# A cached-attention decode kernel: values three groups behind the keys in the load order, and the whole output projection after the last attention group

## The chip, the cores and the metric

The kernel runs on one core of one Trainium2 chip. The metric is the device time of one execution in microseconds. A run counts as slow when it is over 1.5% above the fastest of its kernel. The a runs, the b runs and the c and d runs were made on three different chips; the kernel before was timed beside them each time, at 195.54, 195.39, 195.54 and 195.57 us.

Ratios are means of the fast runs of one kernel over means of the other's in the same call. They are not quite the ratios of the medians that are quoted beside them.

## The reference, cut to what matters

```python
# attention for one new token: B=8, Hq=16, Hkv=8, Dh=256; only the last W=1024 keys count
q = (x @ wq) ...                                    # x [8,448], wq [448,4096]
scores = einsum("bhqd,bhkd->bhqk", q, k) * Dh**-0.5
p = softmax(scores); o = einsum("bhqk,bhkd->bhqd", p, v)
a = o.reshape(B, 1, 4096) @ wo                      # wo [4096,448]
# an MLP on the same x (w1 [448,1792], w2 [1792,448]), and a gate from x and gate_w
out = g * a + (1 - g) * b
```

Keys and values are 8 x 8 x 1024 x 256 bf16 each, 33.5 MB and 33.5 MB. With the weights, 77.68 MB have to be read once, and nothing is used twice. There is little arithmetic per byte.

## The kernel before

The 64 pairs of batch and kv head are cut into 16 groups of four. A group's keys are one slot of 2 MB, its values another. A ring of nine slots is filled by one queue, strictly in the order of `plan`; a slot's next load is issued when the slot has been read.

```python
    RING = 9
    ...
    def pump():
        while len(slots) < min(len(plan), consumed[0] + RING):
            t = ring.tile([P, SLOT], BF16, tag="slot", name="slot")
            plan[len(slots)](t)            # nc.sync.dma_start(...)
            slots.append(t)
    ...
    add_kv("k", A_k_cache, 0, parts=2)     # then w1, wq (two slots), w2
    ...
    for u in range(1, NQ - 1):             # NQ = 16 groups
        add_kv("k", A_k_cache, u)
        if u < NQ - 2:
            add_kv("v", A_v_cache, u - 1)
    add_kv("k", A_k_cache, NQ - 1)
    for u in range(NQ - 3, NQ):
        add_kv("v", A_v_cache, u)
    # then wo: quarters 0 and 1 in one slot, quarters 2 and 3 in the next;
    # quarter 3 is loaded in three pieces, so that the last one is small (224 KB)
```

So the stream ends: key 14, key 15, values 13, 14, 15, output weights. The work on a group is: `transpose_keys` (64 TensorE transposes, copied out by ScalarE and VectorE, with the softmax of the group before woven in), `scores` (16 matmuls), `top` (the maximum), and for an older group `values` (32 matmuls) and `finish` (a fold into `oT`, four matmuls in the trace). `expo`, `turn` and `bring` are the three steps of a group's softmax: exponentials on ScalarE, a transpose on VectorE, and matmuls that put the result in order for `values`.

```python
    for u in range(1, NQ - 1):
        transpose_keys(u, steps(u - 1))
        if u < NQ - 2:
            values(u - 1)
        scores(u)
        top(u)
        if u < NQ - 2:
            finish(u - 1)
    u = NQ - 1
    transpose_keys(u, steps(u - 1))
    scores(u)
    top(u)
    values(u - 2)
    finish(u - 2)
    expo(u)
    turn(u)
    bring(u)
    values(u - 1)
    ...
    finish(u - 1)
    ...
    spread_rows(0, HALF)        # 16 small matmuls: rows of oT for quarters 0 and 1
    values(u)
    finish(u)
    project(0)                  # 32 matmuls of 112 columns a quarter
    spread_rows(HALF, NHQ)
    for q in range(1, NHQ):
        project(q)
    # res = A_ps * gate + mixb, then four small stores
```

## Time and profile before

| | before |
|---|---|
| time, median of 3 runs | 195.49 us (195.32 to 195.64) |
| span in the profile | 193.7 us |
| bytes read | 77.68 MB |
| TensorE busy | 76% of the span |
| last key landed / last weights landed | 165.60 us / 190.02 us |
| last projection matmul done, final vector step begins | 190.43 us, 190.48 us |

From the page: the slices of the span (40 of 4.84 us), the DMA queues, and the chain of work that ended last.

```profile
PEclk9998559999999999999999999999999999999555
DMA  5999999999999999999999999999999999999950
GB/s 203 397 437 415 430 431 428 426 426 416 420 423 430 426 426 423 430 430 423 425 423 423 430 423 416 428 430 420 426 426 430 420 433 420 423 433 404 414 217 10
...
q1 hardware_dynamic: 6512, 77.67, 95.3%
q8 instruction: 18, 0.29, 0.6%
...
DMA 82%; PE 9%; ACT 3%; DVE 2%; issue 1%; SPq 1%; ACTq 0%
```

The DMA row is at 9 tenths in every slice but the first and the last two, at some 425 GB/s. The Trainium skill ("DMA: Bandwidth & Descriptors", Specifications) gives 435 GB/s as the ceiling of the fabric; this trace comes near it: the fastest engine's landings come some 4.9 us apart for 2.097 MB, which is 428 GB/s, though single slices show up to 437. The chain is 82% DMA. The row of the granted TensorE clock falls to 5 tenths near the end, when TensorE begins to have gaps (0.98 us of idle time before 176.95 us, 1.61 us before 179.19 us): it halves at 178.8 us. That is the lower of the two states of "TensorE: Matmul & The Clock Gate" (The two states you'll see); in this trace a values step of 32 matmuls then takes 1.88 us instead of 1.07.

TensorE's timeline at the end, in the kernel before. The columns are the start, the time until the last of the group ends, engine, line, operation, tiles, and in brackets the idle time before it and what ended it.

```profile
174.90 1.07 PE L420 MATMUL PO<-slot,ET 128*8 128x256 bf16 x32
179.83 1.88 PE L420 MATMUL PO<-slot,ET 128*8 128x256 bf16 x32
183.74 1.90 PE L420 MATMUL PO<-slot,ET 128*8 128x256 bf16 x31
186.16 1.02 PE L437 MATMUL sm<-rsel,os__3034 128*128 128x8 f32 x4 [0.52 <-DVE os__3034 L429]
187.11 0.92 PE L563 MATMUL A_ps<-slot,oP 128*8 128x112 bf16 x32
187.97 2.46 PE L563 MATMUL A_ps<-slot,oP 128*8 128x112 bf16 x96
```

These are values 13, 14 and 15, the last fold, and the projection: none of them shows a wait for a transfer. By this view the kernel's end is compute. The records of the DMA semaphores correct it. Each transfer of 128 rows is done by 16 DMA engines, and each engine adds one to the transfer's semaphore. The Trainium skill ("DMA: Bandwidth & Descriptors", Why a DMA increments its semaphore by 16 and not by 1) says that only the full 16 means that all has landed. The last piece of weights was complete at 190.02 us, and the first of the last eight matmuls, which needs it, started at 190.07 us, 0.16 us after the matmul before it. Both the compute and the stream end there.

### The profile page before, as it was taken

To read this page: it belongs to the slowest core of one execution; us is meant where nothing else is said; L and a number is where in the kernel's file an instruction comes from. 1 tells how busy PE (TensorE), PEld (TensorE's weight loads), DVE (VectorE), ACT (ScalarE), POOL (GpSimd) and SP (SyncE) were. 2 spreads that over 40 slices of the span, in tenths; PEclk is the share of its full clock that TensorE was granted. 3 is DMA by queue.
4 is the path that set the end of the run, shared out by engine and by line. 5 is a ranking of instruction groups with operands and counts; after the bars stand their busy time and mean duration, and the time that the engine had idled before them with its cause. 6 is when DMAs were issued, how large, how long until landed. Compare 5 with 4: busy or idle time off the path is not lost.

```text
span 193.7 us, 5200 instructions
## 1 busy us (share of the span) xinstructions
PE 148.1 (76%) x2334; PEld 110.3 (57%) x2334; DVE 112.9 (58%) x259; ACT 82.7 (43%) x101; POOL 0.8 (0%) x7
## 2 busy tenths in 40 slices
PE   1399967777778787878778787878868787984883
PEld 0399936555464646465637373737464646662672
DVE  7532344757475757584847575757565757786320
ACT  2352004536272728181808282828273636582000
POOL 1000000000000000000000000000000000000000
PEclk9998559999999999999999999999999999999555
DMA  5999999999999999999999999999999999999950
GB/s 203 397 437 415 430 431 428 426 426 416 420 423 430 426 426 423 430 430 423 425 423 423 430 423 416 428 430 420 426 426 430 420 433 420 423 433 404 414 217 10
DMA packets 6744, 78.02 MB, mean 403 GB/s; under 512 B 945, under 2 KB 1346, under 8 KB 1986
## 3 DMA queue, kind: packets, MB, share of 16 engines
q1 hardware_dynamic: 6512, 77.67, 95.3%
q8 instruction: 18, 0.29, 0.6%
q10 hardware_dynamic: 210, 0.02, 0.1%
q14 instruction: 4, 0.03, 0.0%
HBM read 77.68 MB, written 0.01 MB: 401 GB/s over the span
## 4 chain that ended last, share of the span: by engine, by line
DMA 82%; PE 9%; ACT 3%; DVE 2%; issue 1%; SPq 1%; ACTq 0%
DMA slot<-in_A_k_cache_dram 77%; DMA slot<-in_B_w_dram 5%; ACT kt L325 2%; PE S_ps L360 2%; PE ktp L322 2%; PE PO L420 2%; PE A_ps L563 2%; ACT E L380 1%; PE sm L437 1%; SPq L107 1%; DVE EB L388 1%; DVE nmx L372 1%; PE sm L399 0%; PE sm L396 0%; PE pp L547 0%
## 5 line engine op out<-in xcount | busy, mean ns | idle before, releaser
L325 ACT COPY kt<-ktp 128x1024 bf16<-128x1024 bf16 x64 | 63.2, 1017 | 82.2 <-PE ktp L322 82.2
L322 PE MATMUL ktp<-ident,slot 128*128 128x128 bf16 x1024 | 70.2, 224 | 22.1 <-ACT kt L325 11.4
L322 PEld LDWEIGHTS <-slot 128*128 128x128 bf16 x1024 | 63.7, 102 | 29.0 <-issue 15.7
L327 DVE COPY kt<-ktp 128x1024 bf16<-128x1024 bf16 x64 | 41.3, 685 | 15.8 <-PE ktp L322 15.6
L372 DVE TENSOR_REDUCE nmx<-S_ps 128x1 f32<-128x1024 f32 x16 | 19.6, 1225 | 22.3 <-PE S_ps L360 22.3
L360 PE MATMUL S_ps<-kt,qw 128*8 128x512 bf16 x256 | 32.3, 627 | 0.3 <-DVE qw L351 0.3
L388 DVE STREAM_TRANSPOSE EB<-E 128x1024 bf16<-128x1024 bf16 x16 | 19.9, 1245 | 6.7 <-ACT E L380 6.5
L420 PE MATMUL PO<-slot,ET 128*8 128x256 bf16 x512 | 18.5, 290 | 6.4 <-DVE ET L401 6.4
L380 ACT ACTIVATE E<-S_ps,nmx 128x1024 bf16<-128x1024 f32 x16 | 17.9, 1120 | 2.4 <-DVE nmx L373 2.4
L420 PEld LDWEIGHTS <-ET 128*8 128x8 bf16 x512 | 12.2, 90 | 10.5 <-DVE ET L401 8.7
L360 PEld LDWEIGHTS <-qw 128*8 128x8 bf16 x256 | 7.3, 95 | 12.0 <-issue 10.4
L401 DVE CAST ET<-sm 128x256 bf16<-128x256 f32 x16 | 6.7, 417 | 0.7 <-PE sm L399 0.7
L396 PE MATMUL sm<-EB,perm 128*128 128x256 bf16 x16 | 4.5, 280 | 1.6 <-DVE EB L388 1.6
L399 PE MATMUL sm<-selr,ones_f 128*128 128x8 f32 x32 | 5.5, 244 | 0.0
L440 DVE CAST oT<-sm 128x16 bf16<-128x16 f32 x16 | 3.5, 221 | 2.8 <-PE sm L437 2.8
L399 PEld LDWEIGHTS sm<-selr,ones_f 128*128 128x128 f32 x32 | 5.0, 196 | 0.1
L339 PE MATMUL qt<-xT,slot 128*128 128x8 bf16 x128 | 3.6, 168 | 0.4 <-DVE z L470 0.4
L339 PEld LDWEIGHTS <-slot 128*128 128x128 bf16 x128 | 3.6, 104 | 0.4 <-issue 0.3
L470 DVE TENSOR_TENSOR z<-hT,b_sb 128x112 f32<-128x112 f32 x1 | 0.3, 275 | 5.3 <-PE hT L460 5.3
L563 PE MATMUL A_ps<-slot,oP 128*8 128x112 bf16 x128 | 3.3, 294 | 0.0
L380 ACT ACTIVATION_READ_ACCUMULATOR E<-S_ps,nmx 128x1 f32 x16 | 3.2, 202 | 0.0
L403 DVE RECIPROCAL rb<-sm 128x8 f32<-128x8 f32 x16 | 3.2, 199 | 0.0
(122 smaller groups left out, 72.2 us busy)
## 6 DMA issues: line engine op xcount, KB each, us to landing
slot<-in_A_v_cache_dram SPq DMA_DIRECT2D x16, 2048.0 KB, 39.3
slot<-in_A_k_cache_dram SPq DMA_DIRECT2D x15, 2048.0 KB, 39.6
slot<-in_A_wo_dram SPq DMA_DIRECT2D x3, 896.0 KB, 32.0
slot<-in_A_k_cache_dram SPq DMA_DIRECT2D x2, 1024.0 KB, 7.2
slot<-in_A_wq_dram SPq DMA_DIRECT2D x1, 2048.0 KB
slot<-in_B_w_dram SPq DMA_DIRECT2D x1, 1568.0 KB
slot<-in_B_w_dram SPq DMA_DIRECT2D x1, 1344.0 KB, 10.1
slot<-in_A_wq_dram SPq DMA_DIRECT2D x1, 1024.0 KB
```

The costliest lines, as they stand in the source:

```text
L322: nc.tensor.transpose(ktp[:, c, :], kn[:, o : o + P], ident[:])
L325: nc.scalar.copy(dst, ktp[:])
L327: nc.vector.tensor_copy(dst, ktp[:])
L339: nc.tensor.matmul(qt[:, k, :], lhsT=w[:, o + c : o + c + P], rhs=xT[:, r + half, :], start=(r == 0 and k == 0), stop=(r == NR), skip_grou ...
L360: nc.tensor.matmul(S_ps[32 * a : 32 * a + RQ, hf * CH * SK : (hf + 1) * CH * SK], lhsT=qw[:, j, b, half, a, :], rhs=KT[hf][:, j, :, a::QUA ...
L372: nc.vector.reduce_max(nmx[:], S_ps[:], axis=AXIS.X, negate=True)
L380: nc.scalar.activation(E[:], S_ps[:], ACT.Exp, bias=nmx[:], scale=1.0, accum_out=rowsum[:])
L388: nc.vector.transpose(EB[:].rearrange("p c r -> p (c r)"), E[:])
L399: nc.tensor.matmul(sm[:, NCK, :], lhsT=ones_f[:], rhs=selr[:], start=True, stop=True)
L401: nc.vector.tensor_copy(ET[:], sm[:, 0:NCK, :])
L420: nc.tensor.matmul(PO[32 * t : 32 * t + RQ, :], lhsT=ET[:, c, 0:RQ], rhs=vn[:, c * Dh : (c + 1) * Dh], start=(c < QUAD), stop=(c >= NCK - ...
L563: nc.tensor.matmul(dst, lhsT=oP[:, j, q, :], rhs=w[:, o + cols.start : o + cols.stop], start=(q == 0 and j == 0), stop=(q == NHQ - 1 and j ...
```

## The change

The intent is to get the last keys earlier. Values give up their places, so that keys run ahead by three groups: the last key moves up by one place (one slot of 2 MB) in the stream, and the long chain from key to scores to softmax starts earlier, while the last three values and the weights still arrive. One small pool is split in two so that the softmax results of three waiting groups fit. The first quarter of the projection, which stood before the second spreading of rows, moves behind it.

```diff
--- before.py
+++ after.py
@@ -64,6 +64,7 @@
     NJ8 = HPQ * NJ
     WO_PARTS = [[(0, NJ8)]] * (NHQ - 1) + [[(0, 4), (4, 6), (6, 8)]]
     RING = 9
+    LAG = 3
     BIG = 1e30
     qscale = float(Dh) ** -0.5
 
@@ -74,7 +75,8 @@
     consts = ctx.enter_context(tc.tile_pool(name="consts", bufs=1))
     ring = ctx.enter_context(tc.tile_pool(name="ring", bufs=RING))
     ktpool = ctx.enter_context(tc.tile_pool(name="ktpool", bufs=4))
-    epool = ctx.enter_context(tc.tile_pool(name="epool", bufs=3))
+    epool = ctx.enter_context(tc.tile_pool(name="epool", bufs=2))
+    opool = ctx.enter_context(tc.tile_pool(name="opool", bufs=LAG + 1))
     ps_s = ctx.enter_context(tc.tile_pool(name="ps_s", bufs=1, space=PSUM))
     ps_kt = ctx.enter_context(tc.tile_pool(name="ps_kt", bufs=3, space=PSUM))
     ps_sm = ctx.enter_context(tc.tile_pool(name="ps_sm", bufs=1, space=PSUM))
@@ -146,12 +148,11 @@
     add(("wq", 0), rows_loader([wq_m[:, 0 : 2 * HD]]))
     add(("wq", 1), rows_loader([wq_m[:, 2 * HD : 3 * HD], wq_t]))
     add(("w2",), rows_loader([w2_v]))
-    for u in range(1, NQ - 1):
+    for u in range(1, NQ):
         add_kv("k", A_k_cache, u)
-        if u < NQ - 2:
-            add_kv("v", A_v_cache, u - 1)
-    add_kv("k", A_k_cache, NQ - 1)
-    for u in range(NQ - 3, NQ):
+        if u >= LAG:
+            add_kv("v", A_v_cache, u - LAG)
+    for u in range(NQ - LAG, NQ):
         add_kv("v", A_v_cache, u)
     for q in range(0, NHQ, 2):
         add(
@@ -397,11 +398,11 @@
             sm[:, 0:NCK, :], lhsT=perm[:], rhs=EB[:, :, 0:RQ], start=True, stop=True
         )
         nc.tensor.matmul(sm[:, NCK, :], lhsT=ones_f[:], rhs=selr[:], start=True, stop=True)
-        ET = epool.tile([P, NCK, RQ], BF16, tag="ET", name="ET")
+        ET = opool.tile([P, NCK, RQ], BF16, tag="ET", name="ET")
         nc.vector.tensor_copy(ET[:], sm[:, 0:NCK, :])
         rb = epool.tile([P, RQ], F32, tag="rb", name="rb")
         nc.vector.reciprocal(rb[:], sm[:, NCK, :])
-        rsel = epool.tile([P, RQ], F32, tag="rsel", name="rsel")
+        rsel = opool.tile([P, RQ], F32, tag="rsel", name="rsel")
         nc.vector.tensor_tensor(rsel[:], rb[:], sel[:], op=ALU.mult)
         soft[u] = (ET, rsel)
 
@@ -516,22 +517,19 @@
     scores(0)
     top(0)
     mlp_out(hs)
-    for u in range(1, NQ - 1):
+    for u in range(1, NQ):
         transpose_keys(u, steps(u - 1))
-        if u < NQ - 2:
-            values(u - 1)
+        if u >= LAG:
+            values(u - LAG)
         scores(u)
         top(u)
-        if u < NQ - 2:
-            finish(u - 1)
+        if u >= LAG:
+            finish(u - LAG)
     u = NQ - 1
-    transpose_keys(u, steps(u - 1))
-    scores(u)
-    top(u)
+    expo(u)
+    turn(u)
     values(u - 2)
     finish(u - 2)
-    expo(u)
-    turn(u)
     bring(u)
     values(u - 1)
     A_ps = ps_misc.tile([P, DQ], F32, tag="misc", name="A_ps")
@@ -572,9 +570,8 @@
     spread_rows(0, HALF)
     values(u)
     finish(u)
-    project(0)
     spread_rows(HALF, NHQ)
-    for q in range(1, NHQ):
+    for q in range(NHQ):
         project(q)
 
     nc.vector.scalar_tensor_tensor(
```

## The prediction

> **What bounds the kernel now.** The DMA. The page's slices show a DMA busy share of 9 tenths in every slice from about 5 to 184 us, at 415 to 435 GB/s; 77.68 MB were read. The Trainium skill ("DMA: Bandwidth & Descriptors", Specifications) puts the fabric ceiling at 435 GB/s, and this trace runs at some 98% of it, so the stream has nothing left to give. The chain of waits is 82% DMA: key-slot transfers of 39.6 us, linked back to back, up to 160.69 us.
>
> After 160.69 us the chain is compute: key group 14 (160.7 to 167.9), key group 15 (to 175.1, 7.14 us each), softmax of 15, values 14, values 15, projection, final vector step at 190.48. That looks like a 30 us compute tail which an earlier last key would shorten. It is the target of the change.
>
> But the transfers' own end lies just under it. The landing records of the DMA semaphores (last of 16 increments) give: last-but-one key 160.70, last key 165.60, values 13, 14, 15 at 170.50, 175.40, 180.33, output weights at 182.52, 184.72, 187.87, then the three pieces of the last quarter at 188.85, 189.44 and 190.02. The final eight projection matmuls carry the wait for that last piece; the first of them starts at 190.07, 0.16 us after the matmul before it. So the old tail already ends on the last byte; only about 0.15 us of stall separates compute from transfer there.
>
> **What the change does.** The bytes, the number of transfers, the ring of nine slots and the instructions' work stay. Values trail keys by three groups, so the last key takes the stream place of the last but one: it lands at about 160.7 instead of 165.6 and its group is processed some 7 us earlier (168 instead of 175 for its scores), less one extra values step (1.05 us) now inside that group. Then values 13 and 14 run as they land; values 15 waits for its landing near 180.3. With the 0.5 clock that idle gaps bring (1.9 us values, 0.4 copy, 1.0 fold, 0.25 copy, spread 0.6) the projection starts near 184.8 instead of 187.1. Moving the first quarter's projection (0.9 us) behind the last group costs nothing: PE then waits for weights at 187.9, 188.9, 189.4 and 190.0. The end stays at last landing plus 0.45 us: about 190.5.
>
> **Early side.** Keys 1, 2, 3 arrive 4.9 us apart while one group takes 7.1, so PE falls some 4 us behind around group 4 and recovers 0.55 us a group (9.25 us work against 9.8 us of arrivals), by about group 11. Slots come free up to 5 us later there, against some 39 us of transfers in flight: no hole in the stream.
>
> **Prediction.** 195.4 us, 8 in 10 between 194.9 and 195.9. Faster by over 2%: 0.02; within 2%: 0.96; slower by over 2%: 0.02.
>
> **What would show it.** DMA slices unchanged and last landing again near 190.0; the last key group 5 to 7 us earlier; PE idle before the projection grows by 2 us or so, put down to output-weight DMA; the final vector step again within 0.3 us of 190.5. A DMA slice below 9 tenths between 30 and 70 us would show a starved stream.
>
> **What would make it wrong.** The 16 DMA engines finish the last piece between 185.2 and 190.0 us; if the new order evens out or worsens this spread, the end moves by it, up to a few us. Or values/keys freed late do stall the issue queue; or the recovery from the early lag is slower than I work out and the compute tail slips past 190 us.

## The result, and the profile after

| | before | after |
|---|---|---|
| time, median (range) of 4 runs each | 195.49 us (195.32 to 195.64) | 195.51 us (195.46 to 195.75) |
| ratio after / before, 95% interval | | 1.0001 (0.9987 to 1.0015) |
| span in the profile | 193.7 us | 193.9 us |

The times are the same. The same views of the kernel after:

```profile
PEclk9999589999999999999999999999999999975555
DMA  5999999999999999999999999999999999999950
GB/s 194 418 426 416 445 424 424 426 426 416 419 426 429 423 423 426 423 431 429 429 426 419 429 426 417 423 426 426 426 429 423 423 416 433 429 429 406 409 202 7
...
q1 hardware_dynamic: 6512, 77.67, 95.1%
q8 instruction: 18, 0.29, 0.6%
...
DMA 86%; PE 6%; ACT 5%; ACTq 1%; issue 0%; DVE 0%; SPq 0%
```

```profile
168.25 0.64 PE L438 MATMUL sm<-rsel,os__2867 128*128 128x8 f32 x4
170.03 1.05 PE L421 MATMUL PO<-slot,ET 128*8 128x256 bf16 x32 [1.14 <-DMA slot<-in_A_v_cache_dram]
174.94 1.88 PE L421 MATMUL PO<-slot,ET 128*8 128x256 bf16 x32
179.85 1.88 PE L421 MATMUL PO<-slot,ET 128*8 128x256 bf16 x32 [0.81 <-DMA slot<-in_A_v_cache_dram]
182.25 1.02 PE L438 MATMUL sm<-rsel,os__3037 128*128 128x8 f32 x4 [0.53 <-DVE os__3037 L430]
183.76 0.93 PE L561 MATMUL A_ps<-slot,oP 128*8 128x112 bf16 x30
185.77 0.92 PE L561 MATMUL A_ps<-slot,oP 128*8 128x112 bf16 x32 [1.07 <-DMA slot<-in_A_wo_dram]
187.95 0.92 PE L561 MATMUL A_ps<-slot,oP 128*8 128x112 bf16 x32 [1.27 <-DMA slot<-in_A_wo_dram]
189.10 0.95 PE L561 MATMUL A_ps<-slot,oP 128*8 128x112 bf16 x24 [0.23 <-DMA slot<-in_A_wo_dram]
190.27 0.36 PE L561 MATMUL A_ps<-slot,oP 128*8 128x112 bf16 x8 [0.22 <-DMA slot<-in_A_wo_dram]
```

The work did move. The projection began at 187.11 us before; now it begins at 183.72 us (the first two of its matmuls are left out above). But everything gained is turned into waits in brackets: for values 13, values 15, and four times for weights. The view of who waits for whom sums the last four to 2.8 us.

The chain of work that ended last shows the same from the other side. Its end before, then after; columns are start, length, and what:

```profile
175.14 1.24 DVE nmx L372
...
179.90 1.84 PE PO L420 x30
...
187.18 0.85 PE A_ps L563 x30
188.03 0.13 PE pp L547 x15
188.15 2.30 PE A_ps L563 x75
```

```profile
130.83 39.15 DMA slot<-in_A_v_cache_dram
...
170.00 20.23 DMA slot<-in_A_wo_dram
190.23 0.04 issue
190.27 0.38 PE A_ps L561 x7
```

Before, all of the chain after 160.69 us is compute (its last 15 us are shown); after, the chain is a transfer up to 190.23 us and then eight matmuls.

When the transfers landed, read from the semaphore records of both traces (first and sixteenth increment, in us from the start of the span):

| transfer | before: first, last engine | after: first, last engine |
|---|---|---|
| key 14 | 156.66, 160.70 | 146.97, 150.37 |
| key 15 | 161.60, 165.60 | 156.78, 160.18 |
| values 13 | 166.48, 170.50 | 166.58, 169.98 |
| values 14 | 171.38, 175.40 | 171.48, 174.90 |
| values 15 | 176.28, 180.33 | 176.39, 179.80 |
| weights, quarter 2 | 182.86, 187.87 | 182.97, 187.91 |
| last piece of quarter 3 | 185.17, 190.02 | 185.28, 190.23 |

The last key came 5.4 us earlier, and the last byte at the same time.

One more thing stands in this table. In both kernels the fastest engine has delivered its share of the last piece by 185.3 us, the slowest not before 190.0 us. The stream ends with one engine, 4.9 us after the first. The experiments follow this too.

### The profile page after: what moved, and what is told of

The parts are those of the page before. It is cut to its first block, busy times and chain, and to the rows that moved or that the text cites. A ratio compares the mean times of both kernels' runs of the same rounds, so it can differ in the third digit from the quotient of the medians.

```text
span 193.9 us, 5200 instructions
## 1 busy us (share of the span) xinstructions
PE 147.3 (76%) x2334; PEld 109.1 (56%) x2334; DVE 112.4 (58%) x259; ACT 82.7 (43%) x101; POOL 0.9 (0%) x7
## 3 DMA queue, kind: packets, MB, share of 16 engines
q1 hardware_dynamic: 6512, 77.67, 95.1%
## 4 chain that ended last, share of the span: by engine, by line
DMA 86%; PE 6%; ACT 5%; ACTq 1%; issue 0%; DVE 0%; SPq 0%
DMA slot<-in_A_k_cache_dram 52%; DMA slot<-in_A_v_cache_dram 20%; DMA slot<-in_A_wo_dram 10%; DMA b_sb<-in_B_b_dram 4%; ACT kt L326 3%; PE ktp L323 3%; PE S_ps L361 2%; ACT E L381 2%; PE PO L421 1%; ACTq L174 0%; PE sm L400 0%; PE A_ps L561 0%; DVE res L577 0%; PE sm L397 0%; ACTq L178 0%
## 5 line engine op out<-in xcount | busy, mean ns | idle before, releaser
L323 PE MATMUL ktp<-ident,slot 128*128 128x128 bf16 x1024 | 69.0, 221 | 23.7 <-DMA slot<-in_A_k_cache_dram 11.7
L323 PEld LDWEIGHTS <-slot 128*128 128x128 bf16 x1024 | 62.7, 100 | 31.0 <-issue 16.6
L561 PE MATMUL A_ps<-slot,oP 128*8 128x112 bf16 x128 | 4.1, 290 | 2.8 <-DMA slot<-in_A_wo_dram 2.8
L561 PEld LDWEIGHTS <-oP 128*8 128x8 bf16 x128 | 2.9, 114 | 3.8 <-issue 3.8
L340 PEld LDWEIGHTS <-slot 128*128 128x128 bf16 x128 | 3.6, 104 | 0.4 <-issue 0.3
```

Source lines behind the costliest of these rows:

```text
L323: nc.tensor.transpose(ktp[:, c, :], kn[:, o : o + P], ident[:])
L340: nc.tensor.matmul(qt[:, k, :], lhsT=w[:, o + c : o + c + P], rhs=xT[:, r + half, :], start=(r == 0 and k == 0), stop=(r == NR), skip_grou ...
L561: nc.tensor.matmul(dst, lhsT=oP[:, j, q, :], rhs=w[:, o + cols.start : o + cols.stop], start=(q == 0 and j == 0), stop=(q == NHQ - 1 and j ...
```

## The experiments

Theory: the end is set by the last byte of the stream; the change shortened the compute tail, and the stream hid it. First rival: the change is neutral because the gain of its order is given back by the later projection. Second rival: the order gains nothing at all.

### a1: the first quarter's projection back in its old place

```diff
     finish(u)
+    project(0)
     spread_rows(HALF, NHQ)
-    for q in range(NHQ):
+    for q in range(1, NHQ):
         project(q)
```

> The changed kernel with one part undone: the first quarter's projection is back before the second spreading of rows. Theory (the last byte of the load stream sets the end): same as the changed kernel, 195.5 us, within 0.3; in the trace the first quarter runs some 0.5 us earlier and the wait for the last weights is longer by as much. Rival (the change gains by its order and gives about as much back by the later projection, 32 matmuls or 0.93 us): 194.6.

Measured: 195.70 us (195.46 to 195.85), ratio to the kernel before 1.0007 (0.9992 to 1.0022). In its trace the projection waits for weights five times instead of four, 3.0 us instead of 2.8. So the move of the projection costs nothing and hides nothing: the first rival falls. That half of the change is idle time put in another place.

### a2 and a3: 2 MB less to load, in both orders

The transfer of values 15 is left out, and the last group reads values 14 again. The result is wrong on purpose (the outputs are close enough that the comparison with the reference did not object). In a2 the edit is made to the kernel before, in a3 to the kernel after.

```diff
-    for u in range(NQ - 3, NQ):          # a3: range(NQ - LAG, NQ)
+    for u in range(NQ - 3, NQ - 1):
         add_kv("v", A_v_cache, u)
...
-        vn = slot("v", u)
+        vn = slot("v", min(u, NQ - 2))
```

> The kernel before with 2 MB less to load: the last values transfer is left out and the last group reads values 14 a second time (wrong result on purpose). Every later transfer should land 4.9 us earlier. Theory: the old order's compute tail ends only 0.16 us after nothing waits, so it is bound by its own chain from the last keys on: 195.3 us (195.1 to 195.5), no longer waiting for any output weights. Rival (bytes alone count in both kernels): 190.6.

> The changed kernel with the same 2 MB left out (wrong result on purpose). Theory: the change did shorten the compute tail and the stream hid it, so here it shows: the projection starts near 183.2 instead of 183.7 and runs through without waiting for weights, some 4 x 0.93 us, to about 187: 192.1 us (191.3 to 192.9), ratio to the same cut of the kernel before 0.984. Rival (the change shortens nothing): equal to the same cut of the kernel before.

| | time, median (range) of 4 | ratio to the kernel before (95%) | last byte in the profiled run |
|---|---|---|---|
| a2, old order | 195.41 us (194.35 to 195.51) | 0.9981 (0.9954 to 1.0007) | 183.80 us |
| a3, new order | 191.62 us (191.57 to 191.91) | 0.9802 (0.9787 to 0.9817) | 185.09 us |

With a shorter stream the old order stays where it was, though its last byte came 6 us earlier: it is bound by its own chain from the last key. The new order is 3.8 us faster by the medians (3.5 us by the means). The second rival falls: the reordering is worth some 3.5 to 3.8 us, in a kernel that has 2 MB less to read. TensorE at the end of a2, then of a3:

```profile
185.55 0.92 PE L563 MATMUL A_ps<-slot,oP 128*8 128x112 bf16 x32
186.25 0.35 PE L547 MATMUL pp<-oT,ident 128*32 128x32 bf16 x16
186.41 2.43 PE L563 MATMUL A_ps<-slot,oP 128*8 128x112 bf16 x96
```

```profile
182.96 3.17 PE L561 MATMUL A_ps<-slot,oP 128*8 128x112 bf16 x126
```

No bracket, no wait for weights, in either. The profiled run of a2 is its fastest (194.35 us), the other three took 195.4. In that run the clock halved at 180.8 us, not at 178.8 as in the profile of before, and values 14 took 1.05 us instead of 1.88. That step alone saved 0.83 us, most of the 1.1 us by which the span of this profile is shorter than that of the kernel before (192.6 against 193.7 us). The link from the clock to the times of the unprofiled runs is argued: they have no trace, and their mean granted clocks over the whole span (0.925 in the fastest run, 0.925 to 0.946 in the others) do not show it.

### a4 and b3: the load stream alone, and the stream with instructions but no work

Why does one engine finish 4.9 us after the first? In the trace of the kernel after, the lag of each engine behind the fastest can be followed from landing to landing. I give it in packets: one row of 16 KB takes an engine 0.612 us. Beside it stands the number of 16 KB instruction fetches (queue q8 of the page, 18 in all) that had begun before the first engine landed.

| landing ends at | q8 fetches so far | engines at least 2.5 packets late | at least 5 late | at least 8 late |
|---|---|---|---|---|
| 17.21 us | 0 | 0 | 0 | 0 |
| 89.98 us | 8 | 8 | 0 | 0 |
| 130.77 us | 12 | 9 | 4 | 0 |
| 174.90 us | 16 | 9 | 8 | 0 |
| 190.23 us | 17 | 9 | 8 | 1 |

Over all the landings of the trace, one more engine is late after each fetch. So each fetch throws one engine back by some 2.6 packets, 1.6 us, and they go round eight of the sixteen engines. The records do not name the engines; this is read from the counts. (The ninth late engine, 3.2 packets behind, follows the 8 KB fetches of queue q14.) The seventeenth fetch, at 180.7 us, is the third for one engine, and that engine ends the kernel.

In a4, all compute is taken out of the kernel after, except one copy of a single column from each slot; loads, order and ring stay. In b3, 63 tiny matmuls per slot are added to that. Their outputs are wrong, which doesn't matter for the times.

```diff
+    for i in range(last):                                # a4
+        nc.vector.tensor_copy(junk[:, i : i + 1], slots[i][:, 0:1])
+        done()
...
+    for i in range(last):                                # b3
+        for _ in range(63):
+            nc.tensor.matmul(pj[0:NB, :], lhsT=slots[i][:, 0:NB],
+                             rhs=slots[i][:, 0:NB], start=True, stop=True)
+        nc.vector.tensor_copy(junk[:, i : i + 1], slots[i][:, 0:1])
+        done()
```

> The changed kernel's load stream with nearly all compute taken out: the same transfers in the same order and ring, one tiny copy per slot, a wrong result on purpose. Theory F: the stream is the floor, and the spread of the 16 DMA engines at its end (first done 185.3, last 190.2 in the changed kernel), which grows in steps of about 1.6 us near each fetch of instructions, comes from those fetches. With some 60 instructions in place of 5200 the spread shrinks to under 1 us and the last landing comes near 185.7: 191.0 us (190.3 to 192). Theory S: the floor is the stream, and the spread belongs to the engines or the data: 195.2 us. Rival to both (slots released late by compute hold the stream back): well under 190.

> The loads alone (190.4 us before) with 63 tiny matmuls per slot added on TensorE, 4664 of its instructions in all against 4507 of the changed kernel, and no other compute (wrong result on purpose). Theory F: about 18 fetches come back and with them the spread: 5.5 to 8 packet times at the last landing, 188.5 to 190.2 us: 193.5 to 195.3 us in time. Rival (the spread comes from the other engines' traffic, which is still missing here): 190.5.

| | time, median of 4 | ratio to before (95%) | last piece: first, last engine | lag of the last engine |
|---|---|---|---|---|
| after | 195.51 us | 1.0001 | 185.28, 190.23 us | 8.1 packets |
| a4, loads alone | 190.42 us | 0.9742 (0.9725 to 0.9758) | 184.88, 185.38 us | 0.8 packets |
| b3, loads and instructions | 194.49 us | 0.9949 (0.9933 to 0.9966) | 184.87, 189.88 us | 8.2 packets |

The DMA queues of a4, then of b3:

```profile
q1 hardware_dynamic: 6512, 77.67, 97.4%
q10 hardware_dynamic: 210, 0.02, 0.1%
q14 instruction: 1, 0.01, 0.0%
```

```profile
q1 hardware_dynamic: 6512, 77.67, 95.4%
q8 instruction: 18, 0.29, 0.6%
```

The first engine ends within 0.4 us of the same time in all three. Without instructions the stream is done 4.9 us earlier. With instructions that do nothing useful, and without the other engines' work, 4.1 us of the 5.1 come back, with 18 fetches and the same pattern of late engines. So the stream is the floor, and about 4.5 us of that floor (last byte at 189.88 us in b3, 185.38 us in a4) is the fetching of the program. b3's first engine ends as early as a4's, so the difference is not a stream held back by slots that were freed late. That a fetch delays one engine is shown; why 16 KB cost it 1.6 us, when a data row of 16 KB takes 0.61, is not. (The record of a fetch packet itself is 1.0 to 1.3 us long.) Two limits of the comparison: a4 and b3 were timed on different chips, each against the kernel before, and b3 brings back its small matmuls together with their fetches.

The Trainium skill ("Runtime: NRT & Kernel Launch", Instruction fetch mechanics) says that the instruction memory is refilled in 16 KiB blocks of 256 instructions through a DMA queue, and that crossing a block boundary is "mostly hidden". The size agrees with the 16 KB packets of queue q8, and one of the 18 fetches comes for about every 259 of the 4668 TensorE instructions in the trace (2334 matmuls, 2334 weight loads). That it is hidden does not hold here: where the DMA engines are the limit, these runs show it in the time.

### b1, b2: fewer instructions

If the seventeenth fetch ends the kernel, a program that needs it later should end earlier. b1 is the kernel after with 408 of its 4507 TensorE instructions saved, by my count of the program, and a correct result. (The traces hold 378 fewer: 2145 matmuls and 2145 weight loads instead of 2334 of each.) Query, second MLP matmul and three quarters of the projection used many matmuls of 8 or 112 columns; they now use matmuls of 448 or 512 columns, with different terms of the sum in the four column groups, which are folded at the end by one small matmul. The core of it, for the projection:

```diff
+            if q < NHQ - 1:
+                t = j % QUAD
+                nc.tensor.matmul(
+                    S_ps[32 * t : 32 * t + NB, 0:D],
+                    lhsT=oP[:, j, q, :],
+                    rhs=w[:, o : o + D],
+                    start=(q == 0 and j < QUAD),
+                    stop=(q == NHQ - 2 and j >= QUAD),
+                )
+                continue
             for dst, cols in quads(A_ps):
                 nc.tensor.matmul(dst, lhsT=oP[:, j, q, :], ...)
+            if j == QUAD - 1:          # part is a copy of S_ps; sel adds its four groups
+                for dst, cols in quads(A_ps):
+                    nc.tensor.matmul(
+                        dst, lhsT=sel[:], rhs=part[:, cols], start=False, stop=False
+                    )
```

b2 is the kernel before with the query and MLP parts of this only (265 instructions fewer by the same count, 250 in the trace), and with its small pool at two buffers for lack of room.

> The changed kernel with the same loads and order and correct result, but 408 fewer TensorE instructions of 4507: query, the second MLP matmul and three quarters of the output projection use wide matmuls in four column groups instead of many narrow ones. Theory F (a fetch of 16 KB of instructions delays one DMA engine by some 1.6 us, and the 17th such fetch is the third one on the engine that finishes last): the 17th fetch comes after about 187 us or not at all, the spread at the last landing falls from 8.1 to about 5.6 packet times (of 0.61 us), the last landing comes near 188.7: 194.0 us (193.6 to 194.5). Rival (the spread comes from compute's own traffic or from the engines): 195.5.

> The kernel before with the query and MLP parts of the same saving (265 TensorE instructions fewer; the projection left as it is, the small pool at two buffers instead of three to make room; correct result). Theory: the 17th fetch comes one group later, near 189 or after, and the stream ends up to 1.5 us earlier, but the compute tail of the old order needs until 190.3 whatever the stream does: 195.3 us (195.0 to 195.6), so that the change is now worth about 0.7%. Rival (the orders are worth the same): equal to the lean changed kernel.

Measured: b1 194.23 us (194.15 to 194.57), ratio 0.9942 (0.9927 to 0.9956); b2 194.83 us (194.50 to 194.87), ratio 0.9965 (0.9950 to 0.9980). The DMA queues of b1:

```profile
q1 hardware_dynamic: 6512, 77.67, 95.9%
q8 instruction: 16, 0.26, 0.6%
```

There were 16 fetches, the last at 178.83 us; no engine was hit three times; the greatest lag was 5.8 packets and the last byte landed at 188.81 us, 1.4 us before that of the kernel after. That is the theory's number. The other traces fit it too. Where the seventeenth fetch began over 4 us before the stream's end (before, after, a1, a3, b3), the greatest lag of the last piece was 7.6 to 8.7 packets; where it came in the last 1.2 us (a2, b2, c1, c2) or not at all (b1, d1), it was 5.6 to 6.6.

b2 missed its expectation by 0.5 us on the fast side. I had taken the old order's compute tail as fixed at 190.3 us. It is not: in b2's trace the last 96 projection matmuls no longer waited for weights (the last eight began at 189.56 us, the last byte had landed at 188.99), and the half-speed clock ended at 189.37 us, so that they took 2.12 us instead of 2.46, and the values step before began 0.26 us earlier.

### c1, c2: the price of the order at a slightly shorter stream

c1 is the kernel after with exactly the saving of b2; c2 is b2 again, beside it.

```diff
# c1: query() and mlp_out() of b1 in the kernel after; project() as in the kernel after
# c2: the kernel b2, unchanged
```

> The changed kernel with exactly the saving of b2_before_lean (query and MLP, 265 TensorE instructions fewer, projection as it was): the clean pair to the lean kernel before, to price the change of order once the stream ends earlier. Theory: last landing 188.8 to 189.4 (the 17th fetch then falls at about 188, when the late engines are nearly done), the projection waits for weights to the end: 194.4 us (194.1 to 194.8), 0.2 to 0.4% under the lean kernel before. Rival (the order is worth nothing at any length of the stream): equal to the lean kernel before, 194.8.

> b2_before_lean once more, beside c1 on the same chip. Theory: 194.8 us again (194.5 to 195.0), with the projection running through without a wait for weights.

Measured, six runs each: c1 194.53 us (194.30 to 195.93), ratio 0.9972 (0.9945 to 1.0000); c2 194.55 us (194.18 to 195.16), ratio 0.9956 (0.9940 to 0.9973). This pair does not show the difference of 0.2 to 0.4% that I expected. Part of the reason stands in c2's trace: the clock halved at 181.1 us instead of 178.8, and the projection ran from 185.89 us on. So early, the old order's tail was held by the stream again: its last eight matmuls began at 189.06 us, just after the last byte at 189.02. Both profiled runs of this pair thus end on the last byte, at 189.02 and 189.04 us, and cannot price the order.

```profile
185.89 0.92 PE L574 MATMUL A_ps<-slot,oP 128*8 128x112 bf16 x32
186.59 0.34 PE L558 MATMUL pp<-oT,ident 128*32 128x32 bf16 x16
186.75 2.66 PE L574 MATMUL A_ps<-slot,oP 128*8 128x112 bf16 x96
```

On c1's side, two of the six runs took 195.64 and 195.93 us. Its seventeenth fetch began at 188.27 us in the profiled run, 0.8 us before the last byte at 189.04. Whether it fell earlier in the two slow ones, and so hit the late engine, I could not see, as only one execution has a trace; the mean granted clock was 0.903 and 0.908 in these two and 0.892 to 0.896 in the other four, which shows that they differed but not how. So at a stream 1 us shorter the value of the order is not settled; at 6 us shorter (a2 and a3) it is clear.

### d1: the lean version once more

```diff
# the kernel b1, unchanged
```

> b1_after_lean once more with more rounds, as it is the version that is to beat both kernels. Theory F: only 16 fetches before the stream ends in every run, so no run near 195.5: 194.2 us (194.0 to 194.6), ratio 0.994. If single runs near 195.6 turn up, as in c1_after_lean_part, a 17th fetch still falls inside the stream at times.

Measured: 194.22 us (193.98 to 194.74, six runs), ratio 0.9935 (0.9918 to 0.9952), 16 fetches, last byte at 188.56 us. No run came near 195.5. This version beats the kernel before by about 0.6%. It was not timed side by side with the kernel after, which took the same time as the kernel before.

### b4: which engines are late

```diff
+    probe = consts.tile([P, 7, 16], BF16)
+    for i, n in enumerate((2, 4, 6, 8, 10, 12, 14)):
+        nc.sync.dma_start(probe[0:n, i, :], A_wo[0:n, 0:16])
```

> The changed kernel with seven transfers of 2, 4, 6, 8, 10, 12 and 14 rows of 32 bytes queued behind the last weights, which use that many of the DMA engines each if the engine count follows the row count; nothing waits for them. It is to tell which engines are the late ones: if they are the first eight, the 8-row probe lands over a spread of 5 to 8 packet times and holds all eight late ones; if the last eight, the 8-row probe lands within 1.2; if every second one, each probe holds late ones in half of its rows. The time should stay within 0.5 us of 195.5.

Measured once: 195.09 us. The probes with 2 and 4 rows landed between 185.0 and 187.1 us, so the engines that serve them are early ones (the trace has one landing for each row; that the same first engines serve every probe is assumed); the probe with 6 rows had one late landing at 188.9 us, and the one with 8 rows two, at 188.2 and 189.1 us. The larger ones were issued too late to tell anything. On that assumption the eight late engines are neither the first eight nor every second one, and a load balanced by hand over the engines, which I had hoped to build on this, was not tried.

## Why the prediction was right

- **The time.** Predicted 195.4 us, 194.9 to 195.9; measured 195.51 us. The reason was the predicted one: a1 shows that no gain was given back, a2 and a3 that the gain is there, 3.8 us, and that the stream covers it.
- **"The stream has nothing left to give."** Right for the rate, too strong for the end. a4 shows that the same 77.67 MB can be done 4.9 us earlier when no program has to be fetched. The prediction named the spread of the engines as a danger, and did not see what makes it. That the last byte landed at nearly the same time in both kernels was therefore in part luck: in both, the seventeenth fetch (185.71 us before, 180.73 us after) came early enough to delay one engine a third time. In b1 it did not come, the last byte landed at 188.81 us, and 194.23 us would have lain below the predicted range.
- **"The last key lands at about 160.7 instead of 165.6."** It landed at 160.18 us. The last group's scores were done by 168.3 us (168 predicted).
- **"The projection starts near 184.8."** It started at 183.72 us, 1.1 us earlier. Half of that is values 15 landing at 179.80 us instead of 180.33; I also had the steps between values and projection a little too long. This fell into idle time. TensorE then also waited for the weights of quarter 1, which landed at 185.72 us; the prediction had its first wait for weights at 187.9 us.
- **"The end stays at last landing plus 0.45 us."** Last landing 190.23 us, final vector step 190.68 us.
- **The early side.** TensorE was to fall 4 us behind at group 4 and recover 0.55 us a group until about group 11. It was 3.2 us behind (key 4 landed at 50.76 us, its transposes began at 53.96) and had caught up at group 7. The term that was mis-sized is the work of a group: I took 9.25 us from the old trace, but in the new order a group takes 8.53 us (group 4 to group 5, 53.96 to 62.49 us). In the old loop the values step waited for the softmax of the group just before (0.49 us each time, 13 times, in the view of who waits for whom), and three groups later it does not. The issue queue did wait for slots, up to 4.9 us at once where it was 0.4 before, and no slice of the DMA row fell below 9.

## What to carry to other kernels

Before reordering a kernel that streams its data once, find out when the last byte lands, from the semaphore records and not from the waits alone: the old kernel's timeline and chain name no wait for weights, and it still ended on the last byte. To learn whether a hidden gain is real, shorten the stream in both versions and compare (a2 and a3). And where the DMA engines are the limit, the program is part of the traffic: 4.1 us came with nothing but instructions (b3 against a4), and the lean program gave 1.2 us (b1) and 1.35 us (d1) against the kernel before of the same call.

## What the Trainium skill lacked or had wrong

- "Runtime: NRT & Kernel Launch", Instruction fetch mechanics: it calls the cost of a fetch mostly hidden. In this DMA-bound kernel every fetch of 16 KB put one DMA engine some 1.6 us behind (lags of about 2.7, 5.3 and 8.1 packets of 0.612 us after one, two and three fetches), and a program of idle instructions with 18 fetches cost 4.1 us of time (194.49 against 190.42 us).
- No page that I read says that the fetches go round eight of a core's sixteen DMA engines, so that a transfer over all sixteen ends with the engine that was hit most: 8 late engines after 16 fetches, one at 8.1 packets after the seventeenth, and 4.9 us between the first and the last engine at the end.
- "TensorE: Matmul & The Clock Gate": the two clock states agree with these traces. The page says of the start of a kernel that the moment of the change differs from run to run; here it matters at the end, where the old order's compute tail met the fall at 178.8, 179.1, 180.8 and 181.1 us in four profiles (before, b2, a2, c2).
